# Softmax attention and soft mixture of experts on one core: the bias of the scores in two products in place of four, and the turned maxima on another path

## The chip, the cores and the metric

The kernel runs on one core of a Trainium2 chip. The metric is the time of one execution on the device in microseconds; of several executions the median is given. Engines are named as the profile names them: PE is TensorE's products, PEld its weight loads, DVE is VectorE, ACT ScalarE, POOL GpSimd, SP SyncE.

## The reference, cut to what matters

```python
# q, k, v: [8, 12, 448, 64] float32
scores = q @ k.T / sqrt(64)
m = max(scores, axis=-1)
e = exp(scores - m)
attn = e / (sum(e, axis=-1) + exp(-m) + 1e-9)        # "softmax off by one"
x = (attn @ v), its heads side by side                # [3584, 768]
logits = x @ phi                                      # [3584, 32]: 8 experts of 4 slots
d = softmax(logits over rows);    slot_input = d.T @ x
slot_out[e] = relu(slot_input[e] @ w1[e]) @ w2[e]     # 768 -> 1024 -> 768
out = softmax(logits over slots) @ slot_out
```

## The kernel before

The attention is worked pair by pair: two heads side by side in the 128 partitions (head 0 in rows 0 to 63, head 1 in rows 64 to 127), 48 pairs, six to a batch entry. Three pairs make a group, for which q, k and v are loaded together. The order of the work is written out by hand: each engine runs its instructions in the order in which the program gives them.

For a pair n:

- `T(n)` turns q and k by 28 small products into a PSUM tile, copied out by ACT (L261) or DVE (L263).
- `A(n, i)` forms the scores with the queries as rows, for the four chunks of queries i (three of 128, one of 64, in which both heads share a tile), in a PSUM tile `ps_a` (products L279, L287, L296). DVE takes the row maxima (L280, L290, L298) into the columns of `mxr`, seven columns to a pair. A runs one to two pairs ahead of the rest.
- `W2(n)` turns the pair's columns of `mxr` by two products (L304) into a PSUM tile `ps_m`; ACT copies it to `mT` (L306), 128 x 128.
- `Bk(n, i)` forms the scores again, now with the keys as rows, in `ps_b` (L337, L366), and subtracts each query's maximum there: `lower` adds products of a column of `sel` (minus one in one row) with the turned maxima `mT`. ACT then takes the exponential (L341, L371).
- `AV(n, ...)` multiplies with the values, a column of ones beside them giving the sum of the exponentials (L405).
- `N1(n)` copies the result out of PSUM (L418, ACT). `EC(g)` takes exp(-m) for a whole group (L311, ACT). `N2(n)` adds the denominator up (L433, DVE), inverts it (L434, DVE) and multiplies on POOL (L438, L448, L449).
- `PX(n)` turns the result for the second half of the kernel (L470; cast L476, ACT).

Every six pairs `P(b)` works on the softmax over phi of one batch entry, in stages that are put between the steps (`post`), some on POOL (L546, L560, L576). `V(g)` puts a group's values in place by four copies on POOL (L377 to L380). POOL also issues the loads: q and k (L176), v (L180, L181), expert weights (L111), staged rows (L143); each of those takes POOL's time too.

The main loop has one step s for each pair, in two half steps y. In step s: scores and bias of pair s; for y = 0 the rest of AV of pair s-1, then `W2(s+1)`, `N1(s-1)`, and when s % 3 = 1 `EC((s-1)//3)`; for y = 1 `T(s+4)`, the start of AV of pair s, `PX(s-2)` and `N2(s-1)` (for the last pairs, on DVE, at y = 0). At the end of a step `slot_loads(s)` follows: V and the loads of v when s % 3 = 0, loads of q and k when s % 3 = 1.

PSUM has three pools in the loop: `psA` with three banks (`ps_a` and the stages of P), `psB` with four (`ps_b`, `ps_m`, `ps_t`, `ps_x`), `psV` with one (`ps_av`).

The large tile W holds the weights of the second half and, in one part of it, the buffers of the loop. Five halves of weights (40 rows of 768 columns) overlap that part and are brought in as buffers fall free (`rows_at`, `load_rows`), some by way of a staged copy in DRAM (`fetch_rows`, on SP, L151). After the loop come the experts and the output.

The bias before, in `lower`: eight products for each key chunk, four to a head:

```python
for i in range(4):
    for hl, o in outs.items():
        c = 2 * i + hl if i < 3 else 6
        nc.tensor.matmul(o[:, i * 128:min(i * 128 + 128, S)], sel[rs[hl], c:c + 1].to_broadcast([64, m]),
                         mT[n][rs[hl], slice(0, 128) if i < 3 else rs[1 - hl]], start=False, stop=True,
                         skip_group_check=True)
```

## Time and profile before

| | us |
|---|---|
| median of three runs | 312.31 |
| their range | 310.15 to 313.27 |
| the profiled execution | 310.94 |
| its span | 309.1 |
| PE busy | 274.8 (89%), 6354 products |
| DVE busy | 251.2 (81%) |
| ACT busy | 251.0 (81%) |
| POOL busy | 184.7 (60%) |
| bias products (L319) | 94.8 busy, 1536 products |
| mean granted clock of PE | 0.962 |

In a line of the profile's groups stand the line of the kernel, engine, operation, what is written from what, the shape and the count; then the busy time of the group in us and the mean duration of one in ns; then the engine's idle time just before them and who ended it. Busy time counts overlapping instructions once, so that busy time over count is less than the mean duration. In the timeline the first number is the start in us from the span's start, the second how long the entry took; xN is N instructions of that line in a row, and square brackets give the idle time before. In the chain of waits each entry is a start, the time it adds to the chain, and the work. A line of the stretches gives, for each engine, busy us and instructions in brackets, then the granted clock, the share of the DMA engines and GB/s.

### The profile page before, as it was taken

The numbers are of one execution on the slowest core, as the hardware profiler recorded it, in microseconds if no ns is written. First come the engines' busy times: TensorE is split into PE (matmuls) and PEld (weight loads), VectorE is DVE, ScalarE is ACT, GpSimd is POOL, SyncE is SP. The second block draws the span as 40 slices with busy tenths as digits, with TensorE's granted clock in tenths as the row PEclk, the third lists the DMA queues.
The fourth block names the chain that finished last, engine by engine and source line by source line (L and its number), as shares of the span: only waits on it lengthen the run. The fifth ranks groups of instructions, "written<-read, shape, count | busy, mean of one in ns | idle before, by whom it ended". The sixth has DMA issues, their size and how long they took to land.

```text
span 309.1 us, 14652 instructions
## 1 busy us (share of the span) xinstructions
PE 274.8 (89%) x6354; PEld 204.6 (66%) x6354; DVE 251.2 (81%) x574; ACT 251.0 (81%) x572; POOL 184.7 (60%) x340
## 2 busy tenths in 40 slices
PE   5999999889899999899899999988998999997730
PEld 3577778677687777678777877767776777662100
DVE  5978899968899898799899999978997996627850
ACT  3599999879799988898899889977996998346730
POOL 8766677767668867875779587837882554000000
PEclk9999999999999999999999999999999999999555
DMA  7999399997999999999999999998999499916997
GB/s 130 187 203 202 45 153 205 182 200 111 194 158 182 148 203 162 188 132 213 149 188 149 209 135 201 152 207 112 199 165 208 73 231 251 292 68 244 405 459 317
DMA packets 47168, 58.82 MB, mean 190 GB/s; under 512 B 2816, under 2 KB 40064, under 8 KB 46848
## 3 DMA queue, kind: packets, MB, share of 16 engines
q0 software_dynamic: 40448, 42.29, 86.8%
q1 hardware_dynamic: 6656, 15.60, 13.3%
q8 instruction: 49, 0.80, 1.0%
q14 instruction: 15, 0.12, 0.1%
HBM read 89.16 MB, written 15.14 MB: 337 GB/s over the span
## 4 chain that ended last, share of the span: by engine, by line
PE 69%; ACT 15%; issue 7%; DVE 5%; DMA 1%; DVEq 0%; ACTq 0%
PE ps_av L405 15%; PE ps_b L319 13%; PE ps_a L279 12%; PE ps_t L254 5%; PE ps_b L366 5%; ACT W L341 4%; ACT W L261 4%; PE ps_b L337 4%; ACT W L371 3%; PE ps_x L470 2%; PE ps_o L865 2%; ACT W L476 2%; PE ps_s L592 2%; PE ps_h L802 2%; DVE mxr L280 2%
## 5 line engine op out<-in xcount | busy, mean ns | idle before, releaser
L280 DVE TENSOR_REDUCE mxr<-ps_a 128x1 bf16<-128x448 f32 x276 | 153.9, 616 | 15.5 <-PE ps_a L279 14.9
L341 ACT ACTIVATE W<-ps_b 128x448 bf16<-128x448 f32 x276 | 134.7, 587 | 7.6 <-PE ps_b L319 5.5
L319 PEld LDWEIGHTS <-sel 64*128 64x128 bf16 (+1 forms) x1536 | 81.8, 98 | 24.2 <-issue 11.5
L319 PE MATMUL ps_b<-mT,sel 64*128 64x128 bf16 (+3 forms) x1536 | 94.8, 211 | 2.1 <-issue 2.1
L279 PE MATMUL ps_a<-W 64*128 64x448 bf16 x276 | 90.9, 359 | 0.5 <-issue 0.2
L337 PE MATMUL ps_b<-W 64*128 64x448 bf16 x276 | 77.6, 357 | 2.4 <-ACT W L261 0.5
L438 POOL TENSOR_TENSOR W<-ubuf,rec 128x384 bf16<-128x384 f32 x45 | 37.1, 825 | 58.1 <-ACT W L476 39.7
L405 PE MATMUL ps_av<-W 128*128 128x65 bf16 (+1 forms) x1536 | 65.3, 196 | 2.8 <-issue 2.8
L405 PEld LDWEIGHTS <-W 128*128 128x128 bf16 (+1 forms) x1536 | 50.2, 100 | 17.0 <-issue 10.5
L476 ACT CAST W<-ps_x 128x512 bf16<-128x512 f32 x47 | 29.0, 616 | 15.1 <-PE ps_x L470 14.5
L254 PE MATMUL ps_t<-ident,W 64*64 64x64 bf16 x1330 | 31.2, 195 | 5.0 <-issue 3.2
L371 ACT ACTIVATE W<-ps_b 128x448 bf16<-128x448 f32 x60 | 34.7, 597 | 0.8 <-PE ps_b L319 0.7
L254 PEld LDWEIGHTS <-W 64*64 64x64 bf16 x1344 | 26.6, 112 | 7.8 <-issue 6.1
L279 PEld LDWEIGHTS <-W 64*128 64x128 bf16 x276 | 25.5, 93 | 8.3 <-issue 0.4
L298 DVE TENSOR_REDUCE mxr<-ps_a 128x1 bf16<-128x448 f32 x48 | 29.6, 618 | 0.1
L418 ACT COPY ubuf<-ps_av 128x455 f32<-128x455 f32 x45 | 27.4, 610 | 0.0
L111 POOL DMA_DIRECT2D W<-in_moe_w_dram x31 | 23.0, 742 | 5.0 <-PE ps_b L319 4.1
L261 ACT COPY W<-ps_t 128x896 bf16<-128x896 bf16 x20 | 19.2, 958 | 4.5 <-PE ps_t L254 4.5
L366 PE MATMUL ps_b<-W 64*64 64x448 bf16 (+1 forms) x108 | 21.3, 372 | 0.1
L449 POOL TENSOR_TENSOR W<-ubuf,rec 128x128 bf16<-128x128 f32 x45 | 18.0, 400 | 3.8
L337 PEld LDWEIGHTS <-W 64*128 64x128 bf16 x276 | 18.3, 94 | 2.6 <-issue 2.2
L296 PE MATMUL ps_a<-W 64*64 64x448 bf16 x96 | 18.9, 382 | 0.1
(145 smaller groups left out, 391.9 us busy)
## 6 DMA issues: line engine op xcount, KB each, us to landing
W<-in_moe_w_dram POOLq DMA_DIRECT2D x24, 768.0 KB, 9.6
W<-in_v_dram POOLq DMA_DIRECT2D x32, 192.0 KB, 5.1
out_dram<-W SPq DMA_DIRECT2D x2, 2688.0 KB, 9.1
W<-in_q_dram POOLq DMA_DIRECT2D x15, 336.0 KB, 5.6
W<-in_k_dram POOLq DMA_DIRECT2D x15, 336.0 KB, 6.8
stage<-in_moe_w_dram POOLq DMA_DIRECT2D x4, 768.0 KB, 10.1
out_dram<-W SPq DMA_DIRECT2D x6, 384.0 KB, 2.6
out_dram<-W SPq DMA_DIRECT2D x3, 768.0 KB, 4.2
```

Of the source, the lines that this page charges most:

```text
L254: nc.tensor.transpose(o, src[r, pl, tok * D:(tok + 1) * D], ident[r, r])
L261: nc.scalar.copy(t, ps)
L279: nc.tensor.matmul(ps[:, 0:S], t[r, 0, i * 128:(i + 1) * 128], t[r, 1, :], start=True, stop=True)
L280: nc.vector.reduce_max(mcol(n, i, hl), ps[:, 0:S], axis=AX.X)
L319: nc.tensor.matmul(o[:, i * 128:min(i * 128 + 128, S)], sel[rs[hl], c:c + 1].to_broadcast([64, m]), mT[n][rs[hl], slice(0, 128) if i < 3 e ...
L337: nc.tensor.matmul(pss[hl][:, 0:S], t[rs[hl], 1, cols], t[rs[hl], 0, :], start=True, stop=False, skip_group_check=True)
L341: nc.scalar.activation(e[:, hl, :], pss[hl][:, 0:S], AF.Exp, scale=scale)
L366: nc.tensor.matmul(outs[hl], t[rs[hl], 1, cols], t[rs[hl], 0, :], start=True, stop=False, skip_group_check=True)
L371: nc.scalar.activation(e, p[:, 0:S], AF.Exp, scale=scale)
L405: nc.tensor.matmul(o, eT[n, i, hl][:, qc], vp[g % 2][:, 2 * pl + hl, i, 0:W65], start=(i == 0 and u == 0 and hl == 0) or (u == 3 and i == ...
L438: eng.tensor_mul(x[:, 0:3, c:c + 128].rearrange("p i (h d) -> p i h d", h=2), u[:, 0:6, 0:D].rearrange("p (i h) d -> p i h d", h=2), rec[: ...
L476: nc.scalar.copy(xT(b, pb), pss[0])
```

## The change

The columns of the turned q are ordered by head: `qcol` puts the shared chunk of 64 queries at 256 for head 0 and at 384 for head 1, in place of 384 for both. The columns of `mxr` are ordered so that the two chunks of a head which follow each other in q stand in neighbouring columns. `W2` turns `mxr` twice, the second time one column further on, into a tile of 256 columns: each row then holds the maxima of two chunks. `lower` so needs two products for each head (256 and 192 columns) in place of four.

`ps_m` moves from `psB` to `psA`, and its copy from ACT (128 columns) to DVE (256 columns). `mT` has two buffers in place of three. As the columns of `mxr` no longer stand in the order of the sums, `EC0` (new, s % 3 = 1, y = 0) puts a group's maxima in order by four copies on POOL, and `EC` takes the exponential from there, at y = 1 of the same step. `N2` runs at y = 1 for all pairs but the last two. The room comes from one row less ("own") in W, so that one row of weights fewer is loaded during the loop; it is fetched after it.

```diff
-    sizes = [("own", 4 * DD), ...
+    sizes = [("own", 3 * DD), ...
-        mxr = pu.tile([128, 2 * NP, 64], BF16, name="mxr")
+        mxr = pu.tile([128, 2 * NP, 66], BF16, name="mxr")
+        def qcol(hl, i):
+            if i < 2:
+                return slice(i * 128, i * 128 + 128)
+            if i == 2:
+                return slice(320, S) if hl == 0 else slice(256, 384)
+            return slice(256, 320) if hl == 0 else slice(384, S)
...
-                    c = kcol(hl, tok) if a else (2 * tok if tok < 4 else 2 * tok - 7) * 64
+                    c = kcol(hl, tok) if a else qcol(hl, tok % 4).start + 64 * (tok // 4)
...
         def mcol(n, i, hl=0):
-            c = 2 * i + hl if i < 3 else 6
+            c = 3 if i == 3 else i if hl else (5, 6, 4)[i]
...
         def W2(n):
-            ps = psB.tile([128, 128], BF16, tag="b", name="ps_m")
-            for r in rs:
-                nc.tensor.transpose(ps[r, :], mxr[:, n % (2 * NP), :], ident)
-            mT[n] = psm.tile([128, 128], BF16, tag="mT", name="mT", bufs=3)
-            nc.scalar.copy(mT[n], ps)
+            ps = psA.tile([128, 256], BF16, tag="a", name="ps_m")
+            for z in range(2):
+                for r in rs:
+                    nc.tensor.transpose(ps[r, z * 128:z * 128 + 128], mxr[:, n % (2 * NP), z:z + 64], ident)
+            mT[n] = psm.tile([128, 256], BF16, tag="mT", name="mT", bufs=2)
+            nc.vector.tensor_copy(mT[n], ps)
+
+        def EC0(g):
+            t = psm.tile([128, NP, 7], F32, tag="nm", name="nm")
+            m = mxr[:, g % 2 * NP:g % 2 * NP + NP, :]
+            nc.gpsimd.tensor_copy(t[:, :, 1:6:2], m[:, :, 0:3])
+            nc.gpsimd.tensor_copy(t[:, :, 0:4:2], m[:, :, 5:7])
+            nc.gpsimd.tensor_copy(t[:, :, 4:5], m[:, :, 4:5])
+            nc.gpsimd.tensor_copy(t[:, :, 6:7], m[:, :, 3:4])
+            st["nm"] = t
 
         def EC(g):
             ec[g] = psm.tile([128, NP, 7], F32, tag="ec", name="ec", bufs=3)
-            z = g % 2 * NP
-            nc.scalar.activation(ec[g], mxr[:, z:z + NP, 0:7], AF.Exp, scale=-scale)
+            nc.scalar.activation(ec[g], st["nm"], AF.Exp, scale=-scale)
 
         def lower(outs, n, m):
-            for i in range(4):
+            for z in range(2):
                 for hl, o in outs.items():
-                    c = 2 * i + hl if i < 3 else 6
-                    nc.tensor.matmul(o[:, i * 128:min(i * 128 + 128, S)], sel[rs[hl], c:c + 1].to_broadcast([64, m]),
-                                     mT[n][rs[hl], slice(0, 128) if i < 3 else rs[1 - hl]], start=False, stop=True,
-                                     skip_group_check=True)
+                    c = (5, 3) if hl == 0 else (0, 2)
+                    src = slice(0, 256) if z == 0 else slice(64, 256) if hl == 0 else slice(0, 192)
+                    nc.tensor.matmul(o[:, 256 * z:min(256 * z + 256, S)], sel[rs[hl], c[z]:c[z] + 1].to_broadcast([64, m]),
+                                     mT[n][rs[hl], src], start=False, stop=True, skip_group_check=True)
...
-        rows_at = {77: 4, 81: 7, 87: 12, 88: 14, 89: 18, 91: 21, 92: 25, 93: 26, 95: 27}
+        rows_at = {77: 3, 81: 6, 87: 11, 88: 13, 89: 17, 91: 20, 92: 24, 93: 25, 95: 26}
...
-                            EC((s - 1) // 3)
-                        if not on_pool(s - 1):
+                            EC0((s - 1) // 3)
+                        if s - 1 >= NPAIR - 2:
                             N2(s - 1)
                 else:
-                    if 0 <= s - 1 and on_pool(s - 1):
+                    if s % 3 == 1:
+                        EC((s - 1) // 3)
+                    if 0 <= s - 1 < NPAIR - 2:
                         N2(s - 1)
...
-        load_rows(rows, 36)
+        load_rows(rows, 35)
...
-        fetch_rows(36, 37)
+        fetch_rows(35, 37)
         fetch_rows(37, 40)
```

`A` and `AV` take their columns of q by `qcol` as well.

## The prediction

> **What bounds the kernel now.** I read the page's groups first, then the stretches of 20 us, then the chain of waits and the timeline around one group of three pairs. Busy time first:

> ```profile
> L280 DVE TENSOR_REDUCE mxr<-ps_a 128x1 bf16<-128x448 f32 x276 | 153.9, 616 | 15.5 <-PE ps_a L279 14.9
> L341 ACT ACTIVATE W<-ps_b 128x448 bf16<-128x448 f32 x276 | 134.7, 587 | 7.6 <-PE ps_b L319 5.5
> ...
> core 0: us, PE busy (x) PEld busy (x) DVE busy (x) ACT busy (x) POOL busy (x), PEclk, DMA share, GB/s
> 90.00:110.00 20.00, 19.62 (x487) 15.42 (x486) 18.41 (x44) 19.06 (x45) 14.21 (x25) 1.00 1.10 171
> ```

> The pair loop runs from the first turned maxima copied (10.4 us) to the last (255.5): 245 us for 47 pairs, 5.2 each. In it three engines are near full: in the stretch shown PE 19.6, ACT 19.1 and DVE 18.4 of 20 us. Over 10 to 250 us the stretches add to 213 of 240 for DVE. A busy ratio of one group is less than its mean duration: 153.9/276 = 0.56 us for a reduction of 616 ns, because neighbours overlap; I cost steps by that rate or from start to start. So little slack is left on any engine, and what lengthens one queue shows. Of the 310.9 us of the profiled execution 309.1 are span; the sum is made on 310.9, which is 1.4 below the median of 312.3.

> **The products.** Does their number cost anything? The chain has both kinds side by side:

> ```profile
> 111.14 0.19 PE ps_b L337 x2
> 111.33 0.20 PE ps_b L319 x8
> ```

> Two score products (448 columns for each head, the heads in different halves of the array) take 0.19 us; eight bias products with the same 448 columns a head take 0.20. The columns set the time, not the count, and the change keeps the columns. At most 0.01 us of each of 192 biases goes: 2 us. Elsewhere the chain shows biases of 0.28 us in two pieces, waiting behind the second head's score, which stays. PE's queue loses 10.6% of its 12,703 instructions (its listing has 11,359); its idle time put down to "issue" by the waits is some 11 us in the loop (L254 3.2, L405 2.8, L319 2.1, L592 1.4, L504 0.9), so 1 us if that goes with the count. Against it stand two more transposes of 128 columns for each pair: 128/448 of 0.19 is 0.05 us, times 48 is 2.6. PE: zero, from -3 to +2.6.

> [...]

> **The copies.** These rows price them:

> ```profile
> L306 ACT COPY mT<-ps_m 128x128 bf16<-128x128 bf16 x48 | 15.1, 315 | 0.5 <-PE ps_m L304 0.2
> L448 POOL TENSOR_SCALAR rec<-halfm,rec 128x2 f32<-128x2 f32 x45 | 12.9, 287 | 0.0
> L380 POOL COPY W<-W 64x192 bf16<-64x192 bf16 x16 | 5.6, 348 | 0.9
> L311 ACT ACTIVATE ec<-mxr 128x21 f32<-128x21 bf16 x16 | 4.7, 291 | 0.0
> L258 DVE COPY W<-ps_k 128x256 bf16<-128x256 bf16 x1 | 0.3, 292 | 0.4 <-PE ps_k L254 0.4
> ```

> ACT's copy of the turned maxima goes. In the timeline ACT's next instruction starts 0.14 us after it (112.68, then 112.82), so ACT gains about 0.15 per pair. DVE's copy has the form of L258, 292 ns; L263 is 0.53 from start to start for 896 columns and L597 0.13 for 128, so 256 are 0.20. From one mT copy to the next the timeline has DVE idle 0.06 us or less in 10 of 47 steps, and ACT never idle in 14. So +0.20 x 10 = +2.0 and -0.15 x 14 = -2.1: zero, with -7 (ACT's in all) and +10 (DVE's in all) as ends. The bank moves from the four of ps_b to the three of ps_a, in the order DVE reads them. The third mT buffer goes without a wait: mT two pairs back was last read in the step before.

> **The wait that is added.** Once per group (s % 3 = 1) the exponentials ec no longer read mxr in the first half step: POOL makes four small copies into nm there, and ACT's exponential stands at the end of the second half step, behind the cast of PX (L476); DVE's L433 directly needs it. In the changed kernel's order POOL's four copies stand behind N2 of the step before, four copies of V and two loads of v. Here is that stretch now:

> ```profile
> 110.19 0.16 DVE L433 SCALAR_TENSOR_TENSOR rec<-ubuf,ec 128x7 f32<-128x7 f32 x1
> ...
> 110.74 0.82 POOL L438 TENSOR_TENSOR W<-ubuf,rec 128x384 bf16<-128x384 f32 x1 [3.83 <-ACT W L476]
> ...
> 114.83 0.59 ACT L476 CAST W<-ps_x 128x512 bf16<-128x512 f32 x1
> 114.90 0.67 POOL L181 DMA_DIRECT2D W<-in_v_dram  x1
> 114.93 0.16 DVE L433 SCALAR_TENSOR_TENSOR rec<-ubuf,ec 128x7 f32<-128x7 f32 x1
> ...
> 115.24 2.27 DVE L280 TENSOR_REDUCE mxr<-ps_a 128x1 bf16<-128x448 f32 x4
> ```

> DVE's L433 of the step before, at 110.19, lets POOL begin; POOL is through its N2, V and v at 115.57, 5.38 us later. In the 13 such groups of the loop (s = 4 to 40) that is 5.4 to 5.9, or 6.1 where P's L576 stands between too; and the next L433 starts 4.5 to 7.3 us after the first. POOL comes later than L433 in 11 of them.

> The four copies show nowhere. The nearest rows are L380 (348 ns for 192 columns, 0.30 to 0.40 from start to start) and L448 (287 ns, 0.38 with the wait behind it); POOL's smallest memsets take 0.10 to 0.17. So 0.25 each, 1.0 in all, with ends at 0.5 and 1.5. Then 0.07 for the signal, 0.29 for the exponential (L311) and 0.05 to DVE. For the group shown: 115.57 + 1.0 + 0.4 = 116.98, where L433 would have stood at 114.93 + 0.20 = 115.13. DVE stands for 1.85 us. The same over the 13 groups (POOL's end plus 1.0, or the end of L476 where that is later, plus 0.4, less L433 plus 0.2) gives 0.6 to 2.6, mean 1.7, together 22; the first group some 2.9, the last two 0.7 each, as no V precedes them. All: 27 us. Without POOL's part L476 alone would leave 0.6 a group, 10 us.

> What is queued behind? On DVE the reductions of the next pair, on ACT its exponentials (until about 116.9 in place of 115.49), on POOL N2. PE has no wait until the three ps_a banks are full: the timeline has score products for the maxima (L279) at 114.73, 115.13, 115.31 and 116.50, so the fourth stops. It would wait for the first reduction, 117.30 + 0.62, and start near 117.95: 1.45 late, of DVE's 1.85. That is 0.78 of the wait, and 27 x 0.78 = 21. I take 2 off for what later gaps of PE and DVE give back. POOL's loads of q and k go 1.5 us later, with four steps to spare.

> **The rest.** N2 of pair 45 moves half a step later, two half steps ahead of its PX: nothing, else 0.4 us once. [...] One row of weights moves from the loop's loads to the end: SP issues three DMAs in place of two at 266 us, 1.1 us each by the 2.18 for two, landing 7 to 8.6 us later, while those rows are read from about 277. Zero; 1 us if that margin is short.

> **Sum.** 310.9 + 0 (PE) + 0 (mT copies) + 21 - 2 (wait) = 330 us, 1.06 of the profiled time. Its own ends: the four copies at 0.5 take 16 x 0.5 x 0.78 = 6 off, 1.5 adds 6; the mT copies -7 to +10; PE -3 to +2.6. Added as squares: about 9 either way, 321 to 340.

> **Rivals.**
> - Faster: the number of products is what PE pays for, and PE alone sets the pace. For: PE is 69% of the chain, L319 13% of it (40 us). If half that went, 20 us would be free; DVE has only 240 - 213 - 10 = 17 in the loop, and the wait must disappear in PE's lead. Half of the 17 gives 302. Against: 0.19 and 0.20 above. [...] 0.12.
> - The wait is mostly swallowed: DVE idles some 27 us in the loop today; if PE, held ahead by full banks, fills that, 27 + 10 (copies) - 27 = 10 is left, less ACT's 4: 317. Against: much of that idle time lies where PE itself is late. 0.15.
> - Everything cancels, within 1%: the four copies run near 0.1 each, and ACT's gain counts fully: 312. 0.08.
> - POOL becomes the bound: copies at 0.38 or more, and each group's N2 late too: 27 + 8 = 35 us of wait in full, 346 less what is regained, about 340. POOL is busy 14 of 20 us, which speaks against more. 0.10.

> **Numbers.** The forecast has 0.55. A measurement tells 1%, some 3 us, from no change. Slower by over 1% (above 315.4): 0.55 + 0.15 + 0.10 = 0.80; within: 0.08; faster: 0.12. The range leaves out the faster rival and half of the top one, and reaches down to the swallowed wait: 314 to 342.

> **What would show it.** DVE's idle time before L433's successor put down to ACT's ec, 16 times, 1 to 2.5 us each, and ACT's ec put down to POOL's nm. Bias products on the chain at 0.19 to 0.20 for four. If biases fall to 0.10 the faster rival holds; if the nm copies take 0.1 each, or DVE's waits at rec sum to under 10 us, my main term is wrong.

## The result and the profile after

The changed kernel takes 326.75 us (median of four runs, 324.95 to 328.37) against 312.31 before: 1.047 times as long, with a 95% interval of 1.039 to 1.055. That is slower, and inside the range of 314 to 342. Medians and ranges here hold every execution, while the ratios leave out those more than 1.5% above the fastest of their kernel. The profiled execution takes 326.64 us, 324.8 of them span, 15.7 more than the one before. From the first turned maxima copied to the last it has 259.6 us (11.1 to 270.7) where the kernel before had 245.1, so that 14.5 of the 15.7 lie in the pair loop.

The groups of the profile's page after, whose lines answer to those of before:

```profile
L288 DVE TENSOR_REDUCE mxr<-ps_a 128x1 bf16<-128x448 f32 x276 | 154.3, 615 | 5.3 <-PE ps_a L287 5.2
L357 ACT ACTIVATE W<-ps_b 128x448 bf16<-128x448 f32 x276 | 131.5, 564 | 12.8 <-PE ps_b L336 7.4
L287 PE MATMUL ps_a<-W 64*128 64x448 bf16 x276 | 91.9, 360 | 20.7 <-DVE mxr L288 20.6
```

DVE's reductions take the same time as before, but they wait less for PE (5.2 us against 14.9). Now PE waits for them: 20.6 us for a bank of ps_a. The stretch of 20 us that was shown before shows all three engines lower (PE 19.6 before, DVE 18.4, ACT 19.1):

```profile
core 0: us, PE busy (x) PEld busy (x) DVE busy (x) ACT busy (x) POOL busy (x), PEclk, DMA share, GB/s
90.00:110.00 20.00, 18.23 (x373) 13.16 (x370) 17.14 (x42) 16.02 (x36) 14.65 (x29) 0.91 0.90 137
```

No engine became the bound: in this stretch each of the three has room, and they wait for each other. The waits say for whom (us in total, times, the longest):

```profile
DVE rec L449 <- ACT ec L328: 22.3, 16, 2.0
PE ps_a L287 <- DVE mxr L288: 20.6, 23, 2.0
ACT ec L328 <- POOL nm L323: 10.2, 13, 1.4
```

DVE stands 22.3 us, once in each of the 16 groups, for the exponentials, and ACT stands 10.2 for POOL's copies. One group, in the chain of waits after (start, what it adds, the work), and then two lines of its timeline:

```profile
118.17 0.66 POOL W L393
...
120.08 0.73 POOL W L180
120.81 0.66 POOL W L181
...
121.52 0.20 POOL nm L320
121.71 0.14 POOL nm L321
121.85 0.13 POOL nm L322
121.97 0.14 POOL nm L323
...
122.13 0.23 ACT ec L328
...
122.39 0.18 DVE rec L449
...
122.79 0.50 DVE mxr L288
...
123.34 0.35 PE ps_a L287
```

```profile
122.39 0.17 DVE L449 SCALAR_TENSOR_TENSOR rec<-ubuf,ec 128x7 f32<-128x7 f32 x1 [1.48 <-ACT ec L328]
...
123.34 0.35 PE L287 MATMUL ps_a<-W 64*128 64x448 bf16 x1 [1.48 <-DVE mxr L288]
```

The chain leaves PE for POOL's copies of V (L393) and the loads of v (L180, L181), goes through the four copies of the maxima, the exponential, DVE's rec and its first reduction, and is back on PE 5.2 us later. PE's score products start at 120.55, 120.94 and 121.13; the fourth waits until 123.34.

### The profile page after: what moved, and what is told of

Read it like the earlier page. It is cut to its first block, busy times and chain, and to the rows that moved or that the text cites. A ratio compares the mean times of both kernels' runs of the same rounds, so it can differ in the third digit from the quotient of the medians.

```text
span 324.8 us, 13414 instructions
## 1 busy us (share of the span) xinstructions
PE 279.5 (86%) x5682; PEld 192.4 (59%) x5682; DVE 260.7 (80%) x622; ACT 245.8 (76%) x524; POOL 193.1 (59%) x403
## 3 DMA queue, kind: packets, MB, share of 16 engines
q1 hardware_dynamic: 6784, 15.80, 12.7%
## 4 chain that ended last, share of the span: by engine, by line
PE 43%; POOL 19%; DVE 13%; ACT 13%; issue 5%; DMA 3%; DVEq 0%; POOLq 0%; ACTq 0%
PE ps_av L421 9%; DVE mxr L288 8%; PE ps_a L287 7%; PE ps_b L336 5%; ACT W L269 3%; POOL W L180 3%; PE ps_b L382 3%; POOL W L393 3%; POOL W L181 3%; PE ps_b L353 3%; POOL W L394 3%; ACT W L492 3%; PE ps_t L262 3%; ACT W L387 3%; PE ps_o L883 2%
## 5 line engine op out<-in xcount | busy, mean ns | idle before, releaser
L357 ACT ACTIVATE W<-ps_b 128x448 bf16<-128x448 f32 x276 | 131.5, 564 | 12.8 <-PE ps_b L336 7.4
L287 PE MATMUL ps_a<-W 64*128 64x448 bf16 x276 | 91.9, 360 | 20.7 <-DVE mxr L288 20.6
L336 PE MATMUL ps_b<-mT,sel 64*128 64x192 bf16 (+3 forms) x768 | 96.2, 262 | 0.0
L353 PE MATMUL ps_b<-W 64*128 64x448 bf16 x276 | 79.3, 361 | 2.5 <-ACT W L269 0.4
L336 PEld LDWEIGHTS <-sel 64*128 64x128 bf16 (+1 forms) x768 | 49.0, 99 | 22.9 <-issue 9.2
L492 ACT CAST W<-ps_x 128x512 bf16<-128x512 f32 x47 | 28.2, 600 | 13.3 <-PE ps_x L486 13.0
L387 ACT ACTIVATE W<-ps_b 128x448 bf16<-128x448 f32 x60 | 32.5, 562 | 1.6 <-PE ps_b L336 1.4
L287 PEld LDWEIGHTS <-W 64*128 64x128 bf16 x276 | 26.2, 95 | 12.4 <-issue 0.9
L262 PEld LDWEIGHTS <-W 64*64 64x64 bf16 x1344 | 29.2, 115 | 3.7 <-ACT W L213 1.6
L306 DVE TENSOR_REDUCE mxr<-ps_a 128x1 bf16<-128x448 f32 x48 | 29.7, 619 | 0.1
L434 ACT COPY ubuf<-ps_av 128x455 f32<-128x455 f32 x45 | 26.0, 577 | 3.2 <-PE ps_av L421 2.8
L449 DVE SCALAR_TENSOR_TENSOR rec<-ubuf,ec 128x7 f32<-128x7 f32 x47 | 7.6, 162 | 22.3 <-ACT ec L328 22.3
L353 PEld LDWEIGHTS <-W 64*128 64x128 bf16 x276 | 18.5, 95 | 2.6 <-issue 1.5
```

Source lines behind the costliest of these rows:

```text
L262: nc.tensor.transpose(o, src[r, pl, tok * D:(tok + 1) * D], ident[r, r])
L287: nc.tensor.matmul(ps[:, 0:S], t[r, 0, qcol(hl, i)], t[r, 1, :], start=True, stop=True)
L306: nc.vector.reduce_max(mcol(n, 3), ps[:, 0:S], axis=AX.X)
L336: nc.tensor.matmul(o[:, 256 * z:min(256 * z + 256, S)], sel[rs[hl], c[z]:c[z] + 1].to_broadcast([64, m]), mT[n][rs[hl], src], start=False, ...
L353: nc.tensor.matmul(pss[hl][:, 0:S], t[rs[hl], 1, cols], t[rs[hl], 0, :], start=True, stop=False, skip_group_check=True)
L357: nc.scalar.activation(e[:, hl, :], pss[hl][:, 0:S], AF.Exp, scale=scale)
```

## The experiments

Ratios are to the kernel before, run beside each on the same chip, with 95% intervals. A difference of two ratios is turned into us with 312. Each interval reaches 0.005 to 0.011 to either side, so that such a difference is known to 2 to 4 us.

**ec from the unordered maxima, on ACT.** The changed kernel without POOL's copies: four exponentials of 9, 6, 3 and 3 columns put the sums in order themselves, at the place of EC0 (y = 0).

```diff
-            nc.scalar.activation(ec[g], st["nm"], AF.Exp, scale=-scale)
+            for dst, src in ((slice(1, 6, 2), slice(0, 3)), (slice(0, 4, 2), slice(5, 7)),
+                             (slice(4, 5), slice(4, 5)), (slice(6, 7), slice(3, 4))):
+                nc.scalar.activation(ec[g][:, :, dst], m[:, :, src], AF.Exp, scale=-scale)
...
-                            EC0((s - 1) // 3)
+                            EC((s - 1) // 3)
```

> The changed kernel, but ec is taken by four small exponentials on ACT straight from mxr, at y = 0 where it stood before; POOL's four copies are gone. If the wait for ec is the loss (22.3 us of DVE's standing, 16 times), some 0.78 of it comes back and ACT gets 16 x 0.4 = 6 us more work, part of it hidden: 309 to 313 us, DVE's wait at rec gone. If the loss lies in the mT copy on DVE, in ps_m's bank or in the second pair of transposes: 320 or more.

304.04 us (302.90 to 304.96), ratio 0.976 [0.971, 0.981]. The wait of rec for ec is gone from the waits, and of PE's 20.6 us for the reductions 1.8 are left:

```profile
PE ps_a L287 <- DVE mxr L288: 1.8, 8, 0.2
PE ps_b L330 <- issue: 0.2, 1, 0.2
```

The added wait so costs 0.0714 of the time, 22 us; the three more exponentials of a group that stand in for POOL's copies are paid for in this. But without it the change is not at zero, as the sum had it: it is 8 us faster than before. The second line is the only entry of PE that these waits put down to "issue"; the next experiment takes it up.

**Eight products again.** The same kernel with each product of a bias cut at 128 columns; everything else of the change stays.

```diff
-                    nc.tensor.matmul(o[:, 256 * z:min(256 * z + 256, S)], ... mT[n][rs[hl], src], ...)
+                    for y in range(0, src.stop - src.start, 128):
+                        nc.tensor.matmul(o[:, 256 * z + y:256 * z + x], ... mT[n][rs[hl], src.start + y:src.start + x], ...)
```

> As e1_ec_on_act, but the bias again in eight products of at most 128 columns per key chunk, with the same columns, order and mT; 768 products and weight loads more, nothing else. If columns set the time: 0 to 3 us above e1_ec_on_act. If each product has an overhead of its own, as the faster rival has it: 10 to 19 us above.

316.99 us (314.35 to 319.49), ratio 1.014 [1.008, 1.020]. Four products in place of eight are worth 0.038, 12 us. Yet a bias costs the same in both, by the chain of waits of the kernel with four products first, and of this one second:

```profile
110.86 0.18 PE ps_b L330 x4
```

```profile
114.36 0.19 PE ps_b L333 x8
```

What differs are stops of PE that no semaphore explains. The waits of the kernel with eight products:

```profile
PE ps_t L262 <- issue: 3.3, 4, 1.1
...
PE ps_av L419 <- issue: 3.0, 6, 0.8
...
PE ps_b L333 <- issue: 1.7, 4, 0.8
PE ps_s L606 <- issue: 1.4, 2, 1.0
```

That view begins an idle time at the modelled end of a product, and so counts less of them. Counted in the trace from one product's start to the next, less the time of its columns, PE stands for more than 0.35 us without a semaphore that ended the wait 17 times from 12 to 262 us with eight products, 12.7 us in all (15.8 with three more that a semaphore ended too), and once with four, 0.4 us. The difference, 12.3, covers the 12 us. The kernel before has 14 such stops, 12.9 us; the changed kernel one, 0.6 us. They fall on any line, the biases among them, and they are the "issue" of PE that the prediction put at "1 us if that goes with the count".

**The same number of instructions, elsewhere.** If the stops come from the number of PE's instructions, they must return when other products are split. Here the biases keep four products and the score products are cut in two halves of 224 columns.

```diff
-                    nc.tensor.matmul(ps[:, 0:S], t[r, 0, qcol(hl, i)], t[r, 1, :], start=True, stop=True)
+                    for c in (0, 224):
+                        nc.tensor.matmul(ps[:, c:c + 224], t[r, 0, qcol(hl, i)], t[r, 1, c:c + 224], start=True, stop=True)
```

> As e1_ec_on_act, with the bias in four products, but every score product (of A and of Bk) in two of 224 columns: again 768 products and weight loads more, now elsewhere and in long products, the result the same. If the 13 us of e2_eight_products come from the number of PE's instructions (PE stops for lack of them, 15 us in the loop there, 1 us in e1_ec_on_act): 313 to 319, with such stops back. If they come from the short bias products themselves: 304 to 307 and no stops.

316.88 us (314.55 to 317.65), ratio 1.017 [1.009, 1.026]: the whole 12 us again, with four products in each bias. The stops are back (11, 12.1 us in all), several of them in places that the cut does not touch:

```profile
PE ps_t L262 <- issue: 3.1, 4, 1.7
PE ps_av L420 <- issue: 2.7, 3, 1.6
...
PE ps_x L485 <- issue: 1.7, 1, 1.7
```

**The kernel before with four products a bias.** One product for each head and half, with one column of `sel` and the turned maxima read twice by a broadcast. It leaves out part of the computation: the second chunk of each head, and the last one in part, get the maxima of the chunk ahead of them.

```diff
-            for i in range(4):
+            for i in range(2):
...
+                    nc.tensor.matmul(o[:, i * 256:i * 256 + 2 * w].rearrange("p (a b) -> p a b", a=2), ...
+                                     mT[n][rs[hl], 0:w].unsqueeze(1).to_broadcast([64, 2, w]), ...)
```

> The kernel before with nothing changed but the number of bias products: two per head, which add the maxima of the first and the third chunk twice (the second and fourth chunk's own are left out), over the same columns. If the number of PE's instructions counts as in e2_eight_products: 297 to 303 and PE's stops without a wait (12.9 us in the loop) nearly gone. If columns alone count: 309 to 312.

299.06 us (297.59 to 299.84), ratio 0.962 [0.955, 0.968]: 12 us from the number of products with nothing else of the change. The stops fall from 14 to 3, 2.7 us.

**POOL's copies put into the kernel before.** EC0 on POOL, EC at y = 1 and N2 at y = 1, as in the change; columns, products and mT as before.

> The kernel before with the path of ec alone changed: four copies on POOL at y = 0, the exponential at y = 1, N2 at y = 1 for all pairs but the last two. If the wait is the loss: 15 to 19 us above the kernel before, 327 to 331 us, with some 20 to 25 us of DVE waiting for ec. If the loss lies elsewhere: 312 to 314.

325.72 us (321.85 to 327.62), ratio 1.041 [1.032, 1.049]. The wait is there in full:

```profile
DVE rec L440 <- ACT ec L319: 23.5, 16, 2.3
...
ACT ec L319 <- POOL nm L314: 8.1, 10, 1.2
```

It costs 12.6 us here and 22 in the changed kernel. Part of it lies where PE stood anyway: PE's stops without a wait fall from 12.9 to 5.4 us. With those 7.5 us given back, 20 of the 23.5 would be felt. That a load passes while PE stands for DVE is argued, not shown.

**V's copies and loads behind N2.** The changed kernel with the copies of V and the two loads of v taken out of POOL's way, called after the next N2.

```diff
+                    if s % 3 == 1:
+                        slot_v(s - 1)
```

> The changed kernel, but the four copies of V and the two loads of v go to POOL one step later, behind the nm copies and N2, so that POOL is free when nm is due; ACT's exponential stays behind the cast of PX. If POOL's queue and ACT's place each hold part of the wait, as the prediction had it: DVE still waits 0.5 to 0.9 us a group, 8 to 14 us in all in place of 22, none of it for POOL, and the time is 313 to 319. If POOL's queue is all of it: 304 to 307. If ACT's place is all of it: 322 or more.

315.03 us (313.61 to 316.47), ratio 1.012 [1.002, 1.023]. ACT's ec waits for nobody any more, and still

```profile
DVE rec L449 <- ACT ec L328: 12.2, 16, 2.2
```

What POOL does ahead of the copies thus costs 0.035, 11 us, of the 22. The rest is put down to ACT, to the exponential's place behind the cast of PX. This run alone does not show that in full: three of PE's stops without a wait are back in its profiled execution, 4.4 us against 0.4 in the first experiment's. The next experiment tries the place by itself.

**ACT's exponentials at y = 1.** The first experiment's kernel, with its four exponentials behind the cast of PX in place of ahead of it; POOL has no part in it.

> As e1_ec_on_act (four exponentials on ACT, nothing on POOL), but at y = 1 behind the cast of PX, where the change has its one. By the same account the place alone leaves DVE 0.6 to 1.0 us a group and ACT 0.4: 311 to 318. If the place costs nothing: 304 to 306, as e1_ec_on_act.

316.7 us (315.19 to 334.86), ratio 1.018 [1.007, 1.028]. The place alone costs 0.042, 13 us, which agrees with the 11 to which the experiment before comes (1.012 less 0.976).

**mT copied by ACT.** The first experiment's kernel with `nc.scalar.copy(mT[n], ps)`.

> As e1_ec_on_act, but the 256 columns of mT are copied by ACT in place of DVE. By the sum (0.20 us less on DVE, 0.25 more on ACT per pair, each felt in a fifth to a third of the pairs): within 4 us of e1_ec_on_act, on either side. If DVE alone sets the pace: 8 to 10 us below it.

307.26 us (306.18 to 308.86), ratio 0.986 [0.981, 0.991]: 3 us worse than on DVE. Of the two engines the change took the better.

**ps_m among ps_b's banks.** The first experiment's kernel with one line undone:

```diff
-            ps = psA.tile([128, 256], BF16, tag="a", name="ps_m")
+            ps = psB.tile([128, 256], BF16, tag="b", name="ps_m")
```

> As e1_ec_on_act, but ps_m back in psB, the pool of four banks in which it stood before; the copy stays on DVE. If its place in the three banks of the maxima costs DVE's queue anything: 1 to 4 us below e1_ec_on_act's 304. If DVE reads it in turn anyway, as the prediction had it: within 1.5 us of it, or above, as the scores then have a bank fewer.

300.74 us (300.47 to 302.33), ratio 0.968 [0.960, 0.975], against 0.976 with the bank of the change: 2.5 us, no more than such a difference is uncertain by. PE's waits for the maxima's banks go from 1.8 us to

```profile
PE ps_a L287 <- DVE mxr L288: 0.2, 1, 0.2
```

**One exponential again.** The columns of mxr put in the order of the sums (head 1 takes the chunks 1, 2, shared, 0, and the sums stand by head), so that ACT's one exponential reads mxr directly at y = 0.

> The four products without the detour of ec: head 0 keeps its columns of q, head 1 has chunks 1, 2, the shared one and 0, so that the seven columns of mxr, from 0 up, are head 0's three, the shared one and head 1's three, neighbours where two follow each other; the sums of AV take the same order, and ec is again one exponential straight from mxr at y = 0. Against e1_ec_on_act three small exponentials per group go, 0.13 us each, 6 us of ACT's time in all: 300 to 304. If ACT is nowhere the limit: 304.

304.45 us (304.11 to 305.59), ratio 0.979 [0.974, 0.984], no better than the four exponentials. ACT's busy time fell by 3 us (247.7 to 244.5), but PE's rose by 5 (274.2 to 278.9). The order swaps the halves of the array that the shared chunk's products use; whether PE loses by that was not tried, so that the price of three small exponentials stays open.

**Copies shared by ACT and DVE.** The kernel just named, with mT copied by ACT in the steps in which DVE copies T.

> As e10_best, but mT is copied by ACT in the steps in which DVE copies the turned q and k, and by DVE where ACT does. By the sum each step's fuller engine loses the 0.20 us: 1 to 4 us below e10_best. If DVE alone or ACT alone is the limit: no gain, or up to 2 us above.

307.42 us (306.77 to 309.06), ratio 0.988 [0.983, 0.994]: 3 us worse. So in the steps in which DVE copies T, too, the copy of mT costs less on DVE.

**One exponential, and ps_m among ps_b's banks.**

> As e10_best with ps_m in psB in place of psA, the step that e9_psm_in_psB makes on e1_ec_on_act. If the place in the three banks of the maxima costs what those two runs suggest: 2 to 4 us below e10_best's 304.5, 300 to 302. If that was scatter between chips: 303.5 to 305.

301.20 us (301.04 to 301.63), ratio 0.972 [0.967, 0.977]: 2.1 us for the bank. Either pair of kernels alone leaves its worth uncertain. Together they speak for some 2 us: in both, each execution with the bank moved is faster than each one without, though the two kernels of a pair ran on different chips. This kernel and that of the bank alone (300.74) beat both the kernel before and the changed one; their intervals overlap.

## Why the prediction came out right, and where it did not

The forecast was 330, or 19.1 above the profiled execution; measured were 0.0471 of 312, 14.7. In the order of its sum:

- **The products, forecast 0 with ends of -3 and +2.6: wrong, -12.** The chain's rows were read rightly. A bias costs 0.18 to 0.20 us with four or eight products, so nothing goes there. The step that failed is the next one, that PE's "issue" time would lose "1 us if that goes with the count". A tenth fewer instructions (12,703 to 11,359 in the listings that the prediction counts) took nearly all of it. It does not fall in proportion: all 14 stops of the kernel before lie where a block of instructions comes late, 2.2 to 2.6 us after its packet starts, as the section on the hardware shows. Two pairs of kernels give the price (eight and four products with the change's columns, and without them), and one with the count put back elsewhere takes it back.
- **The copies, forecast 0 with ends of -7 and +10: +4.** That is what the kernel with eight products stands above the one before (1.014). Some 2 of it are probably the bank of ps_m, which was costed at nothing because the banks come "in the order DVE reads them"; in the waits it shows as 1.8 us of PE standing for the reductions. The remaining 2 hold the second pair of transposes, DVE's longer copy and the three more exponentials that stand in for POOL's copies; they were not told apart, and are within the uncertainty. DVE's copy took 286 ns, as against 292 from the form of L258.
- **The wait, forecast 21 - 2 = 19: 22.** Place and cause are as predicted. Sixteen times DVE stands for ec, 13 times ACT for nm, and it is the fourth score product that stops. POOL was through N2, V and v 5.37 us after the rec before (116.11 to 121.48), where 5.38 was read from the kernel before. Two sizes were off. The four copies took less than half of the 1.0 us:

```profile
L320 POOL CAST nm<-mxr 128x9 f32<-128x9 bf16 x16 | 3.1, 193 | 0.4
...
L323 POOL CAST nm<-mxr 128x3 f32<-128x3 bf16 x16 | 3.0, 186 | 0.0
```

193 to 186 ns each in the groups by form, 0.59 for the four from start to end in the chain (121.52 to 122.11). In the 13 groups that waited for POOL, 0.41 us less takes 5.3 off. The 0.07 and 0.05 us for the signals from POOL to ACT and from ACT to DVE were the author's estimate, and no row of before shows them; the chain after has 0.02 (122.11 to 122.13) and 0.03 (122.36 to 122.39). The forecast's parts (22, 2.9 and twice 0.7) add to 26.3, not 27, and less 5.3 they come near the 22.3 us that DVE stood. And all of it was felt, not 0.78: 22.3 us of standing cost 22, known to 3. PE's waits for the reductions grew by 18.8 (1.8 to 20.6), 0.84 of it. The half clock shown below adds up to 5 us (3 times 3.41 at half speed). That this closes the gap is worked out, not tried.
- **Its split was right.** Without POOL's part the prediction left 10 us of the 27; undoing that part left 12.2 us of standing, and 11 us of time.
- **The rest, forecast 0: it holds.** From the last copy of mT to the end are 54.1 us after and 53.6 before, so the later row of weights cost at most 0.5.
- **The ends.** The ends that the sum names, added as squares, come to 10 us below and 12 above, 320 to 342, where it has 9 on either side. That changes nothing here.

That the sum came within 4.3 us was luck in part. Its main term was right, but its errors have opposite signs: -11.9 for the products, +4.3 for the copies and +3.3 for the wait, -4.3 in all. The three are steps along one row of kernels (before, eight products, four, changed), so that they must add up to what was measured; what checks them are the kernels beside that row, the one before with four products a bias (-12 again) and the two on the exponential's place. Of the rivals, the faster one named the right cause, the number of products, and its 302 is near the 304 of the change without its wait. But it has PE pay for each product, and the wait swallowed, and neither happened: a bias takes 0.18 us in the chain with four products and 0.19 with eight, so that no run here shows a price for each product, nor the 19 us that the expectation for eight products names as its upper end. "Mostly swallowed" (317) falls with PE's 20.6 us, "POOL becomes the bound" with POOL's 59% and its short copies, "everything cancels" with the ratio of 1.047.

What would have shown the failed step beforehand? The waits of the kernel before put 11 us down to "issue", spread over five lines. Setting those moments, line by line, against the DMA queues gives the answer of the last section.

## What to carry to other kernels

Idle time of a full engine with no semaphore behind it is worth a look at what else moves at that time, before it is written off as proportional to something: here 12.9 us of it, 14 stops, went with the loading of the engine's own instructions. A small step that is moved can cost what is queued ahead of it at its new place, on each engine that it passes: four copies of 0.59 us together and one exponential cost 22 us here. And a change that loses can hold one that wins: undoing one part at a time found a kernel 3% faster than before inside one 5% slower.

## What the runs showed of the hardware

**Loads of instructions that stop TensorE.** In the timeline of the kernel before, a bias breaks off after its second product:

```profile
126.62 0.40 PE L319 MATMUL ps_b<-mT,sel 64*128 64x128 bf16 x2
128.15 0.32 PE L319 MATMUL ps_b<-mT,sel 64*128 64x128 bf16 x6 [1.13 <-issue]
```

The view of the DMA queues for the stretch from 125.4 to 126.2 us has one packet on the instruction queue (packets, MB, share); its record starts at 125.59, 2.56 us ahead of the product that goes on:

```profile
q8 instruction: 1, 0.02, 7.6%
```

Each of the 49 packets on that queue in the kernel before has 16,384 bytes. All 14 stops there end 2.2 to 2.6 us after such a packet starts, all 17 of the kernel with eight products 2.2 to 2.4, and all 11 of the one with split scores 2.2 to 2.5. The page of each kernel counts the packets of the whole span; that of the first experiment with eight products comes first, that with four second:

```profile
q8 instruction: 50, 0.82, 1.0%
```

```profile
q8 instruction: 44, 0.72, 0.9%
```

**Half clock after short waits.** The page of the changed kernel gives a mean granted clock of 0.7, 0.7 and 0.8 in three slices of the loop, 0.9 or more in its others. The stretch from 88 to 96 us:

```profile
88.00:96.00 8.00, 7.33 (x137) 5.37 (x137) 6.89 (x17) 5.31 (x13) 5.25 (x9) 0.79 0.92 131
```

In the trace the clock falls to half for 3.41 us each time, at 90.4, 124.5 and 192.8 us (8 us with 3.41 of them at half give 0.79). It falls four times in the kernel before with POOL's copies, once in the middle of the loop with split scores (166.8 us), and never in the loops of the kernel before and of the first experiment. PE's longest single wait in the changed kernel was 2.0 us. With the loops of 13 kernels (all but that with the exponentials at y = 1) cut into steps of the same 3.41 us that end where the clock falls, PE was busy for 0.41 to 0.57 of the step just ahead of each of these eight falls. Five other steps with 0.52 to 0.57 were followed by none, and no fall came after a busier step once the loop was under way. So a low share of work in such a step goes with the fall here; a limit for it was not measured.
